# Sampled key-block copies and key high parts: from GpSimd to the activation engine

## The chip, the cores and the metric

The kernel runs on one core of one Trainium2 chip. The metric is the device time of one execution in microseconds, the median of several runs. A profiled execution records every instruction of the engines: TensorE (PE, with its weight loads as PEld), VectorE (DVE), the activation engine (ACT, also ScalarE), GpSimd (POOL) and SyncE (SP, which here issues all DMAs).

## What is computed

A block-sparse attention over 4 batches, 8 heads, 768 positions in 24 blocks of 32, followed by a feed-forward layer with a rational activation. Every query block sees its own block and both neighbours, the first and the last block, and three sampled blocks; query blocks 0 and 23 see all.

```
mask = np.abs(blk_i - blk_j) <= window
mask = mask | (blk_i == 0) | (blk_j == 0) | (blk_i == n_blocks - 1) | (blk_j == n_blocks - 1)
for qb in range(n_blocks):
    for kb in sampled_blocks[qb]:
        mask[qb * block:(qb + 1) * block, kb * block:(kb + 1) * block] = True
scores = np.where(mask, scores, -1000000000.0)
...
h = x @ w_in
P = a[0] + a[1] * h + a[2] * h2 + a[3] * h3
Q = 1.0 + np.abs(b[0]) * np.abs(h) + np.abs(b[1]) * h2
g = P / (Q + 1e-06)
return (g @ w_out).astype(np.float32)
```

## The kernel before

One program interleaves four kinds of work on the engines.

**Keys and queries.** `prep` and `rest` bring the keys of a batch in six pieces of 128x512. ACT takes each piece's largest magnitude (line 384), DVE makes a scale of it (lines 340 to 352), `split16` writes the high part as float16 (`hl`, the operation recorded at line 151 on GpSimd or DVE and at line 147 on ACT), DVE writes the low part (line 378), PE transposes (line 660), and ACT or DVE moves the result to SBUF. For the first batch the result stays in SBUF in `kall`; for the other three it goes to DRAM (`ks`), and each query block's keys are loaded from there by DMA. Queries have a similar chain (`prep_q`, `hlq`).

**Attention.** `attention` handles one query block. In the first batch, the 22 query blocks that are not 0 or 23 need their three sampled key blocks next to each other: `copies` (lines 826 to 829) reads the three block numbers into registers (line 768) and copies three 128x256 float16 slices out of `kall` into one of two buffers `kx`. The two last slots of both buffers hold blocks 0 and 23 and are filled once by `edges` (line 1072). Then come the scores on PE (line 876), the maxima on DVE (886, 915), the exponentials on ACT (904), transposes on PE (945), their evacuation on ACT (147), and the product with the values on PE (1002).

**Weights.** `weights` and `w_scaled` decode the 64-bit weights: a conversion (lines 147 and 151), three DVE steps (434, 437, 440), a maximum on ACT for `w_in`, and a split in high and low parts (498 and 451 on GpSimd). They feed the units.

**Units.** `unit` takes 256 rows of tokens and 256 columns of the hidden layer: PE at lines 1113 to 1115, ACT at 1120, 1124, 1134, 1141 and 1144, DVE at 1127 to 1158, PE again at 1169 to 1171.

All of it is laid out by a planner, `issue`: every step is an `Op` with an engine, an estimated duration in ns, the steps that it follows, a priority, and the buffers that it takes (`Slot`, `Ring`). The planner repeatedly takes the step that can start first by its own estimates and appends its instructions to its engine's queue; engines then run their queues in order. A step made with `among` has a home engine and others; another engine is chosen where it could start earlier than the home engine by more than a fixed amount (243 ns for GpSimd, 534 ns for ACT, 500 ns for DVE).

Of the kernel before, what the change touches and what calls it, by code (L numbers as in the profile page):

```python
# [23 lines left out]
def kernel(  # L24
# [27 lines left out]
    nc = tc.nc  # L52
# [43 lines left out]
    VE, SC, PO, TE, SY = "DVE", "Activation", "Pool", "PE", "SP"  # L96
# [42 lines left out]
    def among(key, home, **prices):  # L139

        d = {{"ve": VE, "sc": SC, "po": PO}[n]: p for n, p in prices.items()}
        return {home: d[home], **(d if key in ALT else {})}
# [181 lines left out]
    o_setup = Op(VE, 5300, setup, [o_small], prio=-70, uses=[s_work])  # L324
# [183 lines left out]
    kall = const.tile([P, NB, H, BLK], F16, name="kall")  # L508
# [27 lines left out]
    s_kall = [Slot(r_kg) for _ in kgs]  # L536
# [78 lines left out]
    def rest(b, w, j, d, o_scale, sc, prio, before):  # L615
        first = b == 0
        t, g = units[j]
        if first:
            s_ld = d["slot"]
            s_ld.left -= 2  # L620
            o_ld = None
        else:
            d, s_ld = {}, Slot(r_ld)

            def load():
                d["ld"] = new_ld(s_ld)
                load_unit((k, v)[w], b, t, g, d["ld"])

            o_ld = before[w] = Op(SY, [(475, 262144)], load, (), prio - 1, takes=[s_ld], behind=before[w])
        s_hl = Slot(r_hl)  # L630

        def high(eng):
            d["hl"] = new_hl()
            split16(d["ld"], sc[0], d["hl"], w, eng)

        def low():
            split16(d["ld"], sc[0], d["hl"], w, None)

        o = Op(among("k", PO, po=671, ve=396, sc=613) if w == 0 else among("K", PO, po=914, ve=600), 0, high, [o_scale, o_ld], prio, takes=[s_hl], uses=[s_ld])
        o = Op(VE, 663 if w == 0 else 800, low, [o], prio, uses=[s_ld, s_hl])  # L640
        if w == 1:
            def store():
                if kv[b][1] is None:
                    kv[b][1] = scr.tile([S, H * 2 * D], F16, name="vs")
                n = HU * 2 * D
                nc.sync.dma_start(out=kv[b][1][t * CH:(t + 1) * CH, g * n:(g + 1) * n].rearrange("(p s) c -> p s c", s=2),
                                  in_=d["hl"].rearrange("p (s j) a d -> p s (j a d)", s=2))
            v_done[b].append(Op(SY, [(650, 262144)], store, [o], prio, uses=[s_hl, s_scr[b]]))
            return
        on_dve = [first and (j, e) in ((0,1),(1,1),(2,1),(3,1),(4,1),(5,1)) for e in range(2)]  # L650
        ring = r_ph if first else r_sp
        s_ps = Slot(ring)
        if g == 0 and not first:
            s_kt[b] = Slot(r_kt)

        def transposes():
            d["pt"] = (ps_h.tile([P, 512], F32, name="ph") if first else ps_s.tile([P, 512], F32, name="sp")).bitcast(F16).rearrange("p (s h n) -> p s h n", s=2, h=HU)
            for e in range(2):
                for h in range(HU):
                    nc.tensor.transpose(d["pt"][:, e, h], d["hl"][:, 2 * h + e].rearrange("p a d -> p (a d)"), ident16)  # L660

        def evac(e):
            def run(eng):
                if g == 0 and e == 0:
                    kts[b, t] = kgs[t] if first else p1.tile([P, KB, H, BLK], F16, name="kt")
                dst = kts[b, t][:, :, g * HU:(g + 1) * HU].rearrange("p b h (r s) -> p s h b r", s=2)[:, e]
                src = d["pt"][:, e].rearrange("p h (b r) -> p h b r", b=KB)
                times(eng, dst, src, 1.0)
            return run

        def store():
            if kv[b][0] is None:
                kv[b][0] = scr.tile([NB, P, H * BLK], F16, name="ks")
            nc.sync.dma_start(out=kv[b][0][t * KB:(t + 1) * KB].rearrange("b p c -> p b c"), in_=kts[b, t].rearrange("p b h r -> p b (h r)"))

        o = Op(TE, 445, transposes, [o], prio, takes=[s_ps], uses=[s_hl])
        sk = s_kall[t] if first else s_kt[b]
        a = Op(among("e", VE if on_dve[0] else SC, sc=478, ve=598), 0, evac(0), [o], prio, takes=[sk] if g == 0 else [], uses=[s_ps] + ([] if g == 0 else [sk]))
        a.behind = k_evac[b, t][0] if g else None
        c = Op(among("e", VE if on_dve[1] else SC, sc=478, ve=598), 0, evac(1), [o, a], prio, uses=[s_ps, sk])  # L680
        k_evac.setdefault((b, t), []).extend([a, c])
        if g == 1 and not first:
            k_done[b].append(Op(SY, [(475, 524288)], store, k_evac[b, t], prio, uses=[sk, s_scr[b]]))
# [81 lines left out]
    def sampled_rows(x, eng=mybir.EngineType.SP):  # L765

        if (x, eng) not in rows_of:
            rows_of[x, eng] = nc.values_load_multi_w_load_instructions(
                ix[0:1, block(parts[x][1]), 0:NR], engines=[eng], min_val=0, max_val=NB - 1,
                skip_runtime_bounds_check_because="clamped when ix was written")[1]  # L770
        return rows_of[x, eng]
# [12 lines left out]
    kxs = early.tile([P, 2, NR + 2, H, BLK], F16, name="kx", bufs=1)  # L784
# [9 lines left out]
    chain = {}  # L794

    def attention(b, j, prio):
# [7 lines left out]
        w, e4 = (c, e2 // XB), e2 % XB  # L804
# [4 lines left out]
        prio = [prio + 0.05 * m for m in range(n)]  # L809
        omax, oexp, onrm = [], [], []  # L810
        prs = {}
        for m, x in enumerate(xs):
            def one(m, x):
                p = prio[m]
# [4 lines left out]
                h = {}  # L819
                if near and n > 1:  # L820
                    deps += [o for t in range(NCH) for o in k_evac[b, t]]
                    kslots = s_kall
                elif near:
                    s_kx = Slot(r_kx)

                    def copies():
                        rows = sampled_rows(x, mybir.EngineType.Pool)
                        for r in range(NR):
                            nc.gpsimd.tensor_copy(out=kxs[:, s_kx.buf, r].rearrange("p h r -> p (h r)"), in_=kall[:, bass.ds(rows[r], 1)].rearrange("p o h r -> p (o h r)"))

                    a = Op(PO, 1500, copies, [o_setup, chain["edges"]], p - 1, takes=[s_kx], uses=s_kall)
                    deps.append(a)
                    kslots = [s_kx] + s_kall
                else:
                    s_kg = Slot(r_kg)

                    def load():
                        kg, ks, = kgs[s_kg.buf], kv[b][0]
                        flat = kg.rearrange("p s h r -> p s (h r)")
                        if n > 1:  # L840
                            nc.sync.dma_start(out=flat, in_=ks[m * NS:(m + 1) * NS].rearrange("b p c -> p b c"))
                            return
                        nc.sync.dma_start(out=flat[:, 0:3], in_=ks[i - 1:i + 2].rearrange("b p c -> p b c"))
                        if h["new"]:
                            nc.sync.dma_start(out=flat[:, 3 + NR:], in_=ks[0:NB:NB - 1].rearrange("b p c -> p b c"))
                        rows = sampled_rows(x)
                        for r in range(NR):
                            nc.sync.dma_start(out=flat[:, 3 + r], in_=ks[bass.ds(rows[r], 1)].rearrange("o p c -> p (o c)"))

                    def price():  # L850
                        h["new"] = fresh("k", x, s_kg)
                        if n > 1:
                            return [(475, 524288)]
                        l = [(475, 196608)] + ([(475, 131072)] if h["new"] else [])
                        return l + [(860, 65536), (560, 65536), (560, 65536)]

                    a = Op(SY, price, load, [o_setup] + k_done[b], p - 1.95, takes=[s_kg], uses=[s_scr[b]], behind=chain.get("kg"))
                    chain["kg"] = a
                    deps.append(a)
                    kslots = [s_kg]  # L860
# [21 lines left out]
                def maxima():  # L882
                    st = d["st"]
                    add = bias[:, i] if n == 1 else bias[:, 0, 0:1].broadcast_to([P, NS])
                    for g in range(2):
# [5 lines left out]
                o = chain["sc"] = Op(TE, 800 if near else 668, scores, deps, p, behind=chain.get("sc"), takes=[s_sp, s_pr] + ([s_st] if m == 0 else []),  # L891
                                     uses=kslots + [Q["slot"]] + ([] if m == 0 else [s_st]))
# [25 lines left out]
        for m, x in enumerate(xs):  # L918
            s_pr, exps = d[m]
            oexp.append(Op(SC, 1172, exps, [omax], prio[m] + 0.1, takes=[G["s_sm"]] if e4 == 0 and m == 0 else [],  # L920
                           uses=[s_pr, s_st, Q["cslot"]] + ([] if e4 == 0 and m == 0 else [G["s_sm"]])))
# [95 lines left out]
        p = prio[-1] + 3 * 0.1  # L1017
# [301 lines left out]
```

## Time and profile before

| | us |
|---|---|
| median of 3 runs | 892.88 (891.15 to 894.04) |
| profiled execution, its own time | 894.15 |
| span of its instructions | 892.0 |
| PE / DVE / ACT / POOL busy | 828.4 / 743.9 / 653.1 / 157.0 |

The span runs from the first to the last recorded instruction. Busy time is the sum of an engine's instructions; a share taken over the whole span mixes stages with different limits, so the tables by stretch are read first. A "releaser" is what ended the idle time before an instruction.

### The profile page before, as it was taken

To read this page: it belongs to the slowest core of one execution; us is meant where nothing else is said; L and a number is where in the kernel's file an instruction comes from. 1 tells how busy PE (TensorE), PEld (TensorE's weight loads), DVE (VectorE), ACT (ScalarE), POOL (GpSimd) and SP (SyncE) were. 2 spreads that over 40 slices of the span, in tenths; PEclk is the share of its full clock that TensorE was granted. 3 is DMA by queue.
4 is the path that set the end of the run, shared out by engine and by line. 5 is a ranking of instruction groups with operands and counts; after the bars stand their busy time and mean duration, and the time that the engine had idled before them with its cause. 6 is when DMAs were issued, how large, how long until landed. Compare 5 with 4: busy or idle time off the path is not lost.

```text
span 892.0 us, 27246 instructions
## 1 busy us (share of the span) xinstructions
PE 828.4 (93%) x10328; PEld 644.8 (72%) x10328; DVE 743.9 (83%) x1824; ACT 653.1 (73%) x1379; POOL 157.0 (18%) x188
## 2 busy tenths in 40 slices
PE   8988586776999999989999999999999999999997
PEld 3555365565778888777887788878888787788885
DVE  5668999979999888869877788988888887788885
ACT  6668666794788787778876887798758587767563
POOL 2434755736420000100000000200000000000000
PEclk9999798688899999999999999999999999999999
DMA  7799788875776976589655975699557556740000
GB/s 204 188 180 219 175 185 172 183 203 161 188 175 160 250 211 155 149 201 240 176 144 149 264 203 161 156 236 240 152 151 183 145 158 161 174 113 25 1 25 24
DMA packets 238482, 148.02 MB, mean 166 GB/s; under 512 B 16016, under 2 KB 222736, under 8 KB 238352
## 3 DMA queue, kind: packets, MB, share of 16 engines
q1 hardware_dynamic: 238352, 146.29, 65.8%
q8 instruction: 82, 1.34, 0.7%
q14 instruction: 48, 0.39, 0.2%
HBM read 128.92 MB, written 11.01 MB: 157 GB/s over the span
## 4 chain that ended last, share of the span: by engine, by line
PE 61%; DVE 8%; ACT 3%; DMA 3%; SPq 2%; issue 1%; ACTq 0%; DVEq 0%
PE ph L1113 8%; PE acc L1169 8%; PE acc L1171 8%; PE acc L1170 8%; PE ph L1114 7%; PE ph L1115 7%; PE av L1002 5%; PE pt L945 4%; PE sp L876 4%; DMA ld<-in_k_dram 1%; DVE gh L1148 1%; DVE ab L1137 1%; PE sp L733 1%; DVE tt L1154 1%; PE sp L1048 1%
## 5 line engine op out<-in xcount | busy, mean ns | idle before, releaser
L1113 PE MATMUL ph<-xh,wi 128*128 128x256 f16 x768 | 213.2, 278 | 3.8 <-DVE tt L1130 2.6
L1115 PE MATMUL ph<-xh,wi 128*128 128x256 f16 x768 | 212.0, 276 | 2.4 <-POOL wi L498 2.4
L1114 PE MATMUL ph<-xl,wi 128*128 128x256 f16 x768 | 212.0, 276 | 1.0 <-DVE xl L1060 1.0
L904 ACT ACTIVATE pr<-pr,st,cq 128x256 f32<-128x256 f32 x224 | 132.2, 593 | 61.0 <-DVE st L915 54.2
L1169 PE MATMUL acc<-wo_h,gh 128*128 128x512 f32 x384 | 164.9, 429 | 0.0
L1171 PE MATMUL acc<-wo_h,gl 128*128 128x512 f32 x384 | 154.7, 403 | 7.3 <-DVE gl L1158 6.6
L1170 PE MATMUL acc<-wo_l,gh 128*128 128x512 f32 x384 | 154.1, 401 | 1.2 <-POOL wo_l L451 1.2
L1120 ACT ACTIVATE sq<-ph,fc 128x512 f32<-128x512 f32 x96 | 65.3, 680 | 60.2 <-PE ph L1115 59.7
L1137 DVE SCALAR_TENSOR_TENSOR ab<-sq,absb,ab 128x512 f32<-128x512 f32 x96 | 74.1, 772 | 34.3 <-ACT ab L1134 34.0
L151 POOL TENSOR_SCALAR hlq<-ldq,scq 128x512 f16<-128x512 f32 x24 | 23.2, 968 | 445.2 <-DVE scq L352 239.5
L1113 PEld LDWEIGHTS <-wi 128*128 128x128 f16 x768 | 76.2, 99 | 32.2 <-issue 16.5
L886 DVE CUSTOM_DVE_ANT_1 pr<-sp,bias 128x256 f32<-128x256 f32 x224 | 84.6, 418 | 13.8 <-PE sp L876 13.4
L1171 PEld LDWEIGHTS acc<-wo_h,gl 128*128 128x128 f32 x384 | 73.6, 192 | 26.6 <-DVE gl L1158 9.3
L1148 DVE SCALAR_TENSOR_TENSOR gh<-tt,par,rr 128x512 fp32r<-128x512 f32 x96 | 74.9, 780 | 17.1 <-PE acc L1170 13.1
L945 PE MATMUL pt<-ident,pr 128*128 128x128 f32 x448 | 77.1, 294 | 11.8 <-ACT pr L904 7.7
L1115 PEld LDWEIGHTS <-wi 128*128 128x128 f16 x768 | 76.1, 99 | 13.8 <-POOL wi L498 2.9
L1169 PEld LDWEIGHTS acc<-wo_h,gh 128*128 128x128 f32 x384 | 73.9, 192 | 15.7 <-issue 1.2
L945 PEld LDWEIGHTS pt<-ident,pr 128*128 128x128 f32 x448 | 67.4, 206 | 24.7 <-ACT pr L904 10.1
L1170 PEld LDWEIGHTS acc<-wo_l,gh 128*128 128x128 f32 x384 | 73.9, 192 | 14.0 <-POOL wo_l L451 1.8
L1114 PEld LDWEIGHTS <-wi 128*128 128x128 f16 x768 | 76.1, 99 | 9.1 <-issue 1.1
L1002 PE MATMUL av<-vg,pT 128*32 128x64 f32 x3584 | 75.1, 226 | 4.7 <-ACT pT L147 2.5
L1002 PEld LDWEIGHTS av<-vg,pT 128*32 128x32 f32 x3584 | 57.1, 112 | 29.5 <-issue 8.9
(140 smaller groups left out, 1669.3 us busy)
## 6 DMA issues: line engine op xcount, KB each, us to landing
vg<-in_v_dram SPq DMA_DIRECT2D x312, 64.0 KB, 3.3
vg<-in_v_dram SPq DMA_DIRECT2D x88, 192.0 KB, 4.1
vg<-in_v_dram SPq DMA_DIRECT2D x24, 512.0 KB, 5.2
kall<-ks SPq DMA_DIRECT2D x52, 192.0 KB, 2.9
kall<-ks SPq DMA_DIRECT2D x156, 64.0 KB, 2.0
ld<-in_k_dram SPq DMA_DIRECT2D x36, 256.0 KB, 5.5
wl<-in_moe_w_in_dram SPq DMA_DIRECT2D x32, 256.0 KB, 4.8
wl<-in_moe_w_out_dram SPq DMA_DIRECT2D x16, 512.0 KB, 4.1
```

The costliest lines, as they stand in the source:

```text
L886: nc.vector.tensor_tensor_reduce(out=prs[x][:, g].rearrange("p (s r) -> p s r", r=BLK), in0=h["sp"][:, g].rearrange("p (s r) -> p s r", r= ...
L904: nc.scalar.activation(out=prs[x][:, g], in_=prs[x][:, g], func=AF.Exp, scale=Q["c"], bias=st[:, 6 + g:7 + g], accum_out=total if n == 1 e ...
L945: nc.tensor.transpose(pp[:, jj * P:(jj + 1) * P], cols, ident)
L1002: nc.tensor.matmul(av[rows, g], pT[:, 2 * g + kt, rows] if plain else pT[:, 2 * g + kt, pa_, rows], vf[:, g * HG + h4, kt * D:(kt + 1) * D ...
L1113: nc.tensor.matmul(o, wh, xh[:, :, cc], start=(cc == 0), stop=False)
L1114: nc.tensor.matmul(o, wh, xl[:, :, cc], start=False, stop=False)
L1115: nc.tensor.matmul(o, wl, xh[:, :, cc], start=False, stop=(cc == NCC - 1))
L1137: nc.vector.scalar_tensor_tensor(out=d["ab"], in0=d["sq"], scalar=absb[:, 1:2], in1=d["ab"], op0=ALU.mult, op1=ALU.add)
L1148: nc.vector.scalar_tensor_tensor(out=d["gh"], in0=d["tt"], scalar=par[:, 0:1], in1=d["rr"], op0=ALU.add, op1=ALU.mult)
L1169: nc.tensor.matmul(acc[:, t], ghs, wo_h[:, f], start=(new and e == 0), stop=False)
L1170: nc.tensor.matmul(acc[:, t], ghs, wo_l[:, f], start=False, stop=False)
L1171: nc.tensor.matmul(acc[:, t], gls, wo_h[:, f], start=False, stop=(last and e == 1))
```

## The change

The copies of the sampled key blocks are made by the activation engine, which also reads the block numbers into its own registers, and the planner's estimate for the three copies goes from 1500 to 1100 ns. The home engine of the keys' high parts becomes the activation engine; GpSimd and DVE stay allowed for them. `edges` stays on GpSimd.

```diff
-        o = Op(among("k", PO, po=671, ve=396, sc=613) if w == 0 else among("K", PO, po=914, ve=600), 0, high, [o_scale, o_ld], prio, takes=[s_hl], uses=[s_ld])
+        o = Op(among("k", SC, po=671, ve=396, sc=613) if w == 0 else among("K", PO, po=914, ve=600), 0, high, [o_scale, o_ld], prio, takes=[s_hl], uses=[s_ld])
...
-                        rows = sampled_rows(x, mybir.EngineType.Pool)
+                        rows = sampled_rows(x, mybir.EngineType.Activation)
                         for r in range(NR):
-                            nc.gpsimd.tensor_copy(out=kxs[:, s_kx.buf, r].rearrange("p h r -> p (h r)"), in_=kall[:, bass.ds(rows[r], 1)].rearrange("p o h r -> p (o h r)"))
-
-                    a = Op(PO, 1500, copies, [o_setup, chain["edges"]], p - 1, takes=[s_kx], uses=s_kall)
+                            nc.scalar.copy(out=kxs[:, s_kx.buf, r].rearrange("p h r -> p (h r)"), in_=kall[:, bass.ds(rows[r], 1)].rearrange("p o h r -> p (o h r)"))
+
+                    a = Op(SC, 1100, copies, [o_setup, chain["edges"]], p - 1, takes=[s_kx], uses=s_kall)
```

## Rows read from the trace of the kernel before

**Rows 1.** Busy us (count) by stretch: PE, PEld, DVE, ACT, POOL; PEclk, DMA, GB/s.

```profile
100.00:120.00 20.00, 13.21 (x225) 10.39 (x225) 19.90 (x46) 13.67 (x30) 12.49 (x17) 0.74 0.52 127
120.00:140.00 20.00, 17.95 (x216) 13.61 (x218) 19.27 (x37) 10.90 (x24) 10.00 (x11) 1.00 0.90 183
140.00:160.00 20.00, 11.47 (x203) 8.27 (x192) 18.85 (x49) 14.76 (x34) 10.57 (x14) 0.74 0.86 194
160.00:180.00 20.00, 15.34 (x172) 11.81 (x170) 19.37 (x43) 14.48 (x30) 17.01 (x15) 0.67 0.78 173
180.00:200.00 20.00, 15.27 (x189) 12.00 (x187) 14.10 (x30) 18.51 (x41) 5.51 (x6) 0.90 0.77 204
240.00:260.00 20.00, 19.31 (x220) 15.06 (x218) 20.00 (x43) 14.46 (x29) 6.44 (x5) 1.00 0.80 164
500.00:600.00 100.00, 99.55 (x1271) 80.35 (x1273) 85.49 (x211) 83.52 (x180) 8.76 (x9) 1.00 0.76 198
```

**Rows 2.** The chain that ended last, us 190 to 200 and 200 to 260: shares by line.

```profile
by line: ACT pr L904 11.7%; ACT scrap L384 9.8%; issue 9.5%; DVE wi L437 6.9%; ACT wi L147 6.7%; DVE pr L886 6.7%; DVE wi L440 6.2%; ACT dw L147 5.7%; DVE wi L434 4.4%; ACT ld L147 0.4%; DVE st L886 0.2%
...
by line: DVE gl L1158 8.7%; DVE tt L1154 7.7%; DVE dw L437 7.2%; DVE gh L1148 7.1%; DVE dw L440 6.7%; DVE ab L1137 6.5%; DMA kall<-ks 5.8%; issue 5.7%; DVE tt L1127 5.5%; DVE ab L1151 5.0%; DVE fc L1087 5.0%; DVE pr L886 4.0%; DVE dw L434 3
```

**Rows 3.** Instructions of the copies, their block numbers' loads, the high parts: ns min/median/max.

```profile
L829 POOL COPY kx<-kall x66: 392/400/952, 27.3 to 182.3; 128x256 f16 x66
L768 POOLq TENSOR_LOAD <-ix x22: 725/730/946, 26.2 to 175.3; - x22
L151 POOL TENSOR_SCALAR hl<-ld,sc x17: 684/1114/1401, 152.1 to 588.9; 128x512 f16<-128x512 f32 x17
L147 ACT ACTIVATE hl<-ld,sc x1: 722/722/722, 372.6 to 372.6; 128x512 f16<-128x512 f32 x1
```

**Rows 4.** The copies alone (line 829) by stretch: us, POOL busy and count.

```profile
20.00:100.00 80.00, 16.26 (x39) 0.98 0.91 201
100.00:180.00 80.00, 14.55 (x24) 0.79 0.76 169
180.00:200.00 20.00, 2.45 (x3) 0.90 0.77 204
```

**Rows 5.** DVE in order of time, us 148 to 157: start us, us, instruction.

```profile
148.70 0.90 DVE L437 SCALAR_TENSOR_TENSOR wi<-wl,wi 128x512 int32<-128x512 int32 x1
149.65 0.76 DVE L440 SCALAR_TENSOR_TENSOR wi<-wl,wi 128x512 int32<-128x512 int32 x1
150.32 0.88 DVE L1154 SCALAR_TENSOR_TENSOR tt<-tt,par,ab 128x512 f32<-128x512 f32 x1
151.81 0.88 DVE L1158 TENSOR_TENSOR gl<-tt,rr 128x512 fp32r<-128x512 f32 x1
153.28 1.17 DVE L378 SCALAR_TENSOR_TENSOR hl<-ld,sc,hl 128x512 f16<-128x512 f32 x1 [0.59 <-POOL hl L151]
154.72 0.74 DVE L378 SCALAR_TENSOR_TENSOR hl<-ld,sc,hl 128x512 f16<-128x512 f32 x1
155.38 0.68 DVE L437 SCALAR_TENSOR_TENSOR wi<-wl,wi 128x512 int32<-128x512 int32 x1
```

**Rows 6.** GpSimd in order of time: beside Rows 5, and at the first weights.

```profile
148.66 3.49 POOL L829 COPY kx<-kall 128x256 f16 x6 [0.99 <-PE sp L876]
152.13 1.79 POOL L151 TENSOR_SCALAR hl<-ld,sc 128x512 f16<-128x512 f32 x2
...
68.62 1.09 POOL L829 COPY kx<-kall 128x256 f16 x3 [3.64 <-PE sp L876]
69.68 2.04 POOL L151 TENSOR_SCALAR dw<-wi,scw 128x512 f32<-128x512 f32 x3
```

**Rows 7.** ACT groups of the whole span by shape: busy us, mean ns.

```profile
L904 ACT ACTIVATE pr<-pr,st,cq 128x256 f32<-128x256 f32 x224 | 132.2, 593 | 61.0 <-DVE st L915 54.2 <-DVE cq L724 6.6
L147 ACT ACTIVATE wi<-dw 128x512 f16<-128x512 f32 x16 | 9.4, 625 | 0.0
```

**Rows 8.** Waits, us 0 to 100: total us, times, longest.

```profile
POOL kx L829 <- PE sp L876: 10.1, 7, 3.9
```

## What the change should do to the time

> **What bounds the kernel now.** I read the busy time by stretch first, because the share over the whole span (PE 93%) mixes two kernels [rows 1]. From about us 260 on PE is never free: 99.55 of 100 us between 500 and 600. What is left to do there is fixed, so the end moves with the moment at which that state is reached. Between 100 and 260 PE is not the limit. DVE is: it is busy 77.39 of the 80 us from 100 to 180 and all 20 of 240 to 260. Between 180 and 200 the picture turns: DVE falls to 14.10 while ACT is busy 18.51 of 20. Second, the chain of waits: from 200 to 260 its named lines are nearly all DVE, from 190 to 200 ACT holds a third of it (exponentials, weight conversion, maxima) [rows 2]. So before us 260 a microsecond taken from DVE is worth up to a microsecond, one added to ACT costs nothing between 100 and 180, where ACT is idle 26.19 us (80 less 53.81), and costs all of itself between 180 and 200. GpSimd is at 5.5 to 17 of 20 us and bounds nothing by its own time.
>
> The third view is the instructions of the copies: 66, of 392 to 952 ns, median 400 [rows 3]. The spread is the interesting part. In order of time, beside the six copies at us 148.66, DVE instructions with two SBUF inputs are longer than the same ones without GpSimd beside them [rows 5, 6]. GpSimd's work thus costs DVE time, though nobody waits for it by name.
>
> **What is removed.** *The copies.* Between 148.7 and 152.7 DVE's line 437 takes 0.90 us against 0.68 at 155.38, line 440 takes 0.76 against that same 0.68, line 1154 takes 0.88 against the 0.74 of the undisturbed three-operand step at 154.72, and line 1158 takes 0.88, which I set against the 0.68 too [rows 5]. The excess is 0.22 + 0.08 + 0.14 + 0.20 = 0.64 us beside six copies, 0.107 us for each. In the DVE-bound stretch and the one after it lie 24 + 3 = 27 copies [rows 4]; 27 x 0.107 = 2.9 us of DVE. The other 39 come before us 100, where DVE has room; nothing is counted for them. Bounds: 0, if DVE merely waits elsewhere, and 27 x 0.40 = 10.8, if every copy held DVE for its undisturbed length. I stay at 2.9, the row that stands beside copies.
>
> The trace shows DVE and GpSimd lengthening each other, and only in some pairs. The Trainium skill (GPSIMD Engine Reference, 8. Key points) says that the two share SBUF interfaces and contend when the DVE instruction has two SBUF inputs or runs in a two-port mode; taken as full exclusion that would give an estimate of 10.8 in place of 2.9 us, and the rows with 0.76 and 0.88 speak for the smaller number.
>
> *The high parts.* Six of the 18 later ones lie between 152 and 180. At 153.28 a DVE low part takes 1.17 us against 0.74 beside two high parts on GpSimd [rows 5, 6]: 0.43 for two, 1.3 us for six. Bounds 0 and 6 x 0.69 = 4.1. The twelve of the batches after that fall in the PE-bound part, where only 0.45 of 100 us are to be had [rows 1]; I take 0.5 us for both, 0 to 0.9. The six of the first batch (before us 24) change engine at about equal price, and are counted at nothing: ACT's evacuations of the transposed keys cover or collide with them, by at most one instruction, 0.72 us either way.
>
> *GpSimd's queue.* The copies at 68.62 had waited 3.64 us for PE's scores, and the scaling of the first weights stands behind them until 69.68 [rows 6]. Over the first 100 us such waits sum to 10.1 us [rows 8]. Freed, those weights start up to 1.1 us sooner. I take nothing, since ACT's own copies then stand in front of ACT's part of the same weights.
>
> **What is added.** *Copies on ACT.* No row shows one. Nearest below: half of a 128x512 conversion of 625 ns, 0.31 us; above: the 128x256 exponential of 593 ns [rows 7]. I take 0.40, the undisturbed length on GpSimd and between the ends; three are 1.2 us. Each group of three needs a load of its block numbers, 730 ns of the queue [rows 3]; on GpSimd it ran while earlier copies did. Bounds 0 and 0.73 for each group; I take 0.2. So 1.4 us for a group (0.93 to 2.5), 22 groups, 31 us on ACT. Eight groups, 11.2 us, fall between 100 and 180 into 26.19 us of idle ACT: cost nothing, as long as they find the gaps. One, at 180, falls where ACT is the limit: 1.4 us on the path. In front of us 100 are 13 groups, 18 us; the ends of that stretch are DMA arrivals, and I count nothing.
>
> For the copy itself the Trainium skill (VectorE: DVE Perf Modes, The TRN2 errata) gives ScalarE 224 cycles and one for each element at 1.2 GHz from SBUF to SBUF, an estimate of 0.40 us; no run shows it yet, and the sum would be the same by it.
>
> *High parts on ACT.* 722 ns for the one that ACT already does, against 684 to 1401 on GpSimd [rows 3]. The six take 4.3 us of the same idle 26.19: 15.5 with the copies. GpSimd is chosen whenever it can start 243 ns sooner, so some will stay there; the gain of 1.3 shrinks with them.
>
> *The new wait.* A copy waits until PE has done with its buffer. On GpSimd those 10.1 us [rows 8] held up GpSimd alone. On ACT, whatever is queued behind waits too: exponentials and evacuations, for which PE waits, and conversions and maxima of the weights, for which DVE waits.
>
> **The sum.** Gains 2.9 + 1.3 + 0.5 = 4.7, cost 1.4, net 3.3 us. The profiled time of 894.15 becomes 890.85 (span 888.7). That execution lies 1.27 above the median of 892.88, so the median becomes 889.6, 0.37% faster. About 0.3%, 2.7 us, is what a measurement of this kernel can tell from no change.
>
> **The rivals.** *ACT becomes the bound: slower.* Place: us 100 to 200. ACT's idle time there is broken into pieces that come before results of DVE; a group of 1.4 us, put ahead of something that DVE needs, delays DVE, which has only 2.61 idle us in 80 to catch up. At stake are 11.2 + 4.3 + 1.4 = 16.9 us. Where half of it is exposed, 8.45 less the gain of 4.7 is 3.75 us: 896.6. Where all of the copies are and no high part, 12.6 - 4.7 = 7.9: 900.8. It decides from 4.7 / 16.9 = 28% exposure on. For it: ACT at 67% goes to 87% of 100 to 180 (15.5 more in 80), and queues run in order. Against it: ACT stays below DVE's 97%, and the planner knows the 1100 ns.
>
> *The gain is given back: no difference.* The planner finds ACT fuller and hands weight conversions to GpSimd, which lengthens DVE again. At 0.215 us each (0.43 for two) ten conversions return 2.2 of the 3.3 us: 891.8. For it: GpSimd has just been freed.
>
> *The high parts don't move.* ACT is rarely free within 243 ns, and nearly all 18 stay on GpSimd. The gain is 1.8 smaller: 891.4, no measurable difference. It is possible because the edit changes a preference alone.
>
> *DVE is freed by more.* If copies held DVE at twice the row's rate, 2.9 more: 886.7. It counts with the forecast, as faster.
>
> **How the numbers follow.** Forecast 0.40, of which 0.10 with the larger relief; ACT as the bound 0.30; given back 0.18; high parts unmoved 0.12. Hence faster 0.40, within 0.3% 0.30, slower 0.30: two mechanisms of nearly equal size stand against each other, and which one wins is not much better than open. The range for the measured time is 884 to 901: the low end takes 2.9 more for the copies and some of the weights and the high parts' upper bound; the high end is that of all copies exposed. The likeliest case's own range is 886 to 891.5.
>
> **What would show it.** The profile after should have 66 ACT copies of about 0.40 us, GpSimd busy some 35 to 55 us less than 157, and DVE's lines 437, 440, 1154 and 1158 with fewer long instances between 100 and 180. The forecast is right if DVE stays above 95% there and PE reaches its full state about 3 us sooner. It is wrong if DVE's idle time between 100 and 200 grows beyond the 8.5 us of now, with ACT's exponentials, conversions or evacuations as the releasers, or if copies on ACT wait for PE's scores with those behind them. If GpSimd's busy time falls by less than the copies' 33 us, work has come back to it.

## The result, and the profile after

The changed kernel takes 888.87 us (median; 885.71 to 893.16) against 894.05 of the kernel before: ratio 0.9935, 95% interval 0.9911 to 0.9959. A second measurement, among the experiments, gave 0.9906 (0.9875 to 0.9937). Both intervals lie below 1: it is faster, by 0.65% and 0.94%; 0.37% was forecast.

The first profile is of the longest of the nine executions (893.16 us), so the readings below are from the second, of 887.19 us. The page first: the span, and each engine's busy us and instructions.

```profile
span 885.4 us, 27256 instructions
...
PE 825.7 (93%) x10349; PEld 645.1 (73%) x10349; DVE 738.2 (83%) x1825; ACT 672.5 (76%) x1444; POOL 118.9 (13%) x122
```

GpSimd has 38 us less than 157.0, ACT 19 us more than 653.1, DVE 5.7 us less than 743.9. The first profile has a span of 891.4 us and the same busy time of DVE, 738.2: the two profiles of this one kernel end 6.0 us apart. Next the copies, the loads of their block numbers and the high parts of the later batches, which answer to [rows 3] (ns min/median/max, first and last start).

```profile
L829 ACT COPY kx<-kall x66: 388/402/419, 26.7 to 195.2; 128x256 f16 x66
...
L768 ACTq TENSOR_LOAD <-ix x22: 696/702/2027, 25.1 to 192.4; - x22
...
L147 ACT ACTIVATE hl<-ld,sc x5: 698/706/724, 157.3 to 563.0; 128x512 f16<-128x512 f32 x5
...
L151 POOL TENSOR_SCALAR hl<-ld,sc x13: 692/857/1964, 168.3 to 582.1; 128x512 f16<-128x512 f32 x13
```

On ACT all copies are alike, 388 to 419 ns, where they ranged from 392 to 952 on GpSimd. Of the 18 later high parts five are now on ACT, where one was before, and of the first batch's six two: GpSimd has lost six high parts in all. In turn the weights' conversions went the other way: in the groups of line 151 GpSimd now makes 25 of them (wo_h 9, wi 8, dw 8), seven more than before.

Last the busy time by stretch, for [rows 1] (PE, PEld, DVE, ACT, POOL, then PEclk, DMA, GB/s); the last line is of the kernel before.

```profile
100.00:180.00 80.00, 54.03 (x874) 43.97 (x873) 73.50 (x167) 66.56 (x155) 34.94 (x30) 0.92 0.89 192
180.00:200.00 20.00, 20.00 (x206) 15.83 (x204) 17.48 (x44) 15.95 (x37) 3.42 (x5) 0.88 0.59 164
200.00:260.00 60.00, 50.08 (x660) 38.45 (x657) 60.00 (x136) 44.78 (x95) 25.39 (x21) 0.94 0.67 183
...
200.00:260.00 60.00, 51.01 (x578) 39.04 (x577) 59.77 (x129) 38.32 (x79) 29.24 (x23) 0.89 0.69 176
```

Between 100 and 260 DVE is idle for 6.5 + 2.52 + 0 = 9.0 us, against 2.61 + 5.90 + 0.23 = 8.7 before: not less. ACT rose from 53.81 to 66.56 in the first 80 us and fell from 18.51 to 15.95 in the 20 after them.

### The profile page after: what moved, and what is told of

The parts are those of the page before. It is cut to its first block, busy times and chain, and to the rows that moved or that the text cites. A ratio compares the mean times of both kernels' runs of the same rounds, so it can differ in the third digit from the quotient of the medians.

```text
span 891.4 us, 27256 instructions
## 1 busy us (share of the span) xinstructions
PE 826.2 (93%) x10349; PEld 645.1 (72%) x10349; DVE 738.2 (83%) x1825; ACT 672.4 (75%) x1444; POOL 119.8 (13%) x122
## 4 chain that ended last, share of the span: by engine, by line
PE 60%; DVE 13%; DMA 11%; SPq 6%; ACT 5%; issue 3%; POOL 1%; ACTq 0%; POOLq 0%; DVEq 0%
PE acc L1169 8%; PE ph L1113 8%; PE acc L1171 7%; PE acc L1170 7%; PE ph L1115 7%; PE ph L1114 7%; PE av L1002 5%; PE pt L945 4%; PE sp L876 4%; DMA ldq<-in_q_dram 4%; DMA vg<-in_v_dram 3%; DVE tt L1127 1%; DMA ld<-in_k_dram 1%; ACT scrap L384 1%; SPq L972 1%
## 5 line engine op out<-in xcount | busy, mean ns | idle before, releaser
L1115 PEld LDWEIGHTS <-wi 128*128 128x128 f16 x768 | 75.6, 98 | 9.7 <-POOL wi L498 0.4
```

The source lines that it names most:

```text
L1115: nc.tensor.matmul(o, wl, xh[:, :, cc], start=False, stop=(cc == NCC - 1))
```

## The experiments

**What was asked.** The prediction takes the gain from work that changes engines, which relieves DVE (theory 1 in the expectations). A rival to that arose with the result: the planner lays out everything anew for any change of its inputs, and of two programs with the same work one may simply have the better plan (theory 2). Theory 3 says that GpSimd's queue, freed of the copies, has the weights ready sooner. An engine can be exchanged without touching the plan: the step is planned as before and only its instructions go into another queue. That separates the two.

**The two halves of the change.** The copies alone:

```diff
 among("k", PO, po=671, ve=396, sc=613)
-nc.gpsimd.tensor_copy(...)
+nc.scalar.copy(...)
-Op(PO, 1500, copies, ...)
+Op(SC, 1100, copies, ...)
```

> The copies go to the activation engine, the key high parts keep GpSimd as home; the planner lays the program out anew. Theory 1 (DVE is relieved of GpSimd's copies): most of the gain is here, 2.9 of 4.7 us by the prediction, so 0.994 to 0.998 of the kernel before. Theory 2 (the gain comes from the order that the planner happened to make): any value between 0.99 and 1.01, unrelated to the share of GpSimd work removed. Theory 3 (GpSimd's queue is freed, weights are ready sooner): like theory 1, with the first unit's matmuls at least 1 us sooner than 81.5 us.

Measured 1.0057 (1.0035 to 1.0079). The half that should have held most of the gain makes the kernel slower.

The high parts alone:

```diff
-among("k", PO, po=671, ve=396, sc=613)
+among("k", SC, po=671, ve=396, sc=613)
```

> Only the home engine of the key high parts changes; the copies stay on GpSimd. Theory 1 (relief of DVE): small, at most 1.8 us of gain, and less as only a few high parts move: 0.998 to 1.000. Theory 2 (order): any value between 0.99 and 1.01, as the planner's order changes throughout for an edit that moves a handful of instructions.

Measured 0.9890 (0.9858 to 0.9922): a gain as large as the whole change's within the intervals, from the half that takes six instructions of 0.7 us off GpSimd. Neither result fits the sum. Theory 2 had set 0.99 to 1.01 for both: the first lies in it, the second just below it by its median. So wide a range is weak support; the exchanges that follow decide more.

**The engine exchanged, the plan kept.** First, copies on ACT in the plan of the kernel before:

```diff
-nc.gpsimd.tensor_copy(...)
+nc.scalar.copy(...)
 Op(PO, 1500, copies, ...)
```

> The copies are issued on the activation engine, but the planner still plans them as GpSimd steps of 1500 ns with GpSimd as home of the high parts: the queues of PE, DVE and SyncE keep exactly the order of the kernel before, only the copies and their register loads sit in ACT's queue at the place where they were planned for GpSimd. Theory 1 (relief of DVE by fewer GpSimd instructions): 1 to 4 us faster than before, 0.9955 to 0.999, DVE busy time down by 3 to 4 us. Theory 2 (the order of the changed kernel is what is faster): no gain, 1.000 to 1.008, as the order is the old one and ACT has 27 us more to do. Rival of the prediction (copies block ACT): slower by over 0.3%, with ACT idle before the copies until PE's scores.

Measured 1.0011 (0.9985 to 1.0037): no gain that can be told. Then copies on GpSimd in the plan of the changed kernel:

```diff
-nc.scalar.copy(...)
+nc.gpsimd.tensor_copy(...)
 Op(SC, 1100, copies, ...)
```

> The reverse: the order of the changed kernel on PE, DVE and SyncE to the instruction, high parts placed as in the changed kernel, but the copies are issued on GpSimd. Theory 1 (relief): the gain of the copies is gone, the time lies 2 to 4 us above the changed kernel, 0.996 to 1.000 of the kernel before. Theory 2 (order): the gain stays or grows, since ACT is also spared 27 us: 0.985 to 0.994 of the kernel before. Theory 3 (GpSimd's queue): above the changed kernel by 2 us or more, with scaling of weights on GpSimd late behind the copies.

Measured 0.9939 (0.9915 to 0.9964). The plan of the changed kernel, with its moved high parts, brings a gain with the copies where they were before; against 0.9935 and 0.9906 of the changed kernel itself, the engine of the copies makes no difference that these intervals can tell. They don't exclude one of up to about 3 us (0.9939 less 0.9906). Theory 3 falls as well: in this run the first unit's matmuls start at 72.0 us, as in the changed kernel (72.1) and not as in the kernel before (81.5), though the copies stand in GpSimd's queue.

```profile
L1113 PE MATMUL ph<-xh,wi x768: 269/273/421, 72.0 to 877.1; 128*128 128x256 f16 x192
...
L1113 PE MATMUL ph<-xh,wi x768: 269/273/422, 72.1 to 868.1; 128*128 128x256 f16 x192
...
L1113 PE MATMUL ph<-xh,wi x768: 269/273/421, 81.5 to 874.7; 128*128 128x256 f16 x192
```

The lines are this run's, the changed kernel's and that of the kernel before. The earlier first weights are the plan's doing, not the freed queue's.

**The changed kernel again,** without an edit, beside the next three:

> The changed kernel once more, on the same chip and against the same runs of the kernel before as the three next to it, with a new profile. If the gain is a property of the program: 0.991 to 0.996 again. The new profile should show in which stretch of the span the gain lies; the first profile, at 893.16 us, was the longest of nine executions.

Measured 0.9906 (0.9875 to 0.9937), a little more than was expected. The gain is a property of the program.

**Another plan, no engine changed by the edit.** One estimate of the planner in the kernel before:

```diff
-a = Op(PO, 1500, copies, ...)
+a = Op(PO, 1400, copies, ...)
```

> Kernel before with one number changed: the planner's estimate for the three copies on GpSimd is 1400 instead of 1500 ns. No work changes its engine, no instruction is added or removed but PE's filling matmuls; only the order of the queues comes out otherwise. Theory 2 (the order decides, as a lottery): the time moves by more than 0.3% either way, within 0.985 to 1.01. Theory 1 (engines' work decides): 0.998 to 1.002.

Measured 1.0102 (1.0071 to 1.0134). And one constant of the planner's choice:

```diff
-slack, fend, f00, fgap = 21.0, 80000, 3000, 0
+slack, fend, f00, fgap = 25.0, 80000, 3000, 0
```

> Kernel before with one constant of the planner changed: of two steps the one of smaller priority is preferred if it starts at most 25 ns (21 before) later. No work changes engine by edit; a second sample of what another order alone does. Theory 2 (order as a lottery): off by more than 0.3% in either direction, within 0.985 to 1.015. Theory 1 (engines' work alone decides): 0.998 to 1.002.

Measured 1.0080 (1.0047 to 1.0113). Neither edit says that any work changes its engine; only the planner's free choices (order, and the engine of the steps that may go to several) come out otherwise (GpSimd has 182 and 187 instructions in these runs, 188 before). They cost 1.0% and 0.8%, and in both cases the change is far larger than the 0.2% that theory 1 allowed. What a plan costs shows in the stretches of the first one's profile:

```profile
100.00:180.00 80.00, 56.20 (x840) 43.94 (x843) 74.97 (x164) 53.49 (x117) 46.82 (x52) 0.81 0.83 165
180.00:200.00 20.00, 12.05 (x136) 9.47 (x126) 16.60 (x24) 15.03 (x30) 6.67 (x5) 0.74 0.78 219
200.00:260.00 60.00, 49.90 (x561) 38.04 (x562) 54.68 (x132) 40.87 (x86) 26.28 (x23) 0.89 0.63 173
```

DVE's idle time from 100 to 260 is 5.03 + 3.40 + 5.32 = 13.75 us, against 8.7 before and 9.0 after, so this plan loses 5 us in the stretch that DVE bounds. Its longest waits from 180 to 262 have no common cause; below the three dots stand two of the kernel before:

```profile
DVE wi L434 <- ACT wi L147: 2.1, 1, 2.1
DVE gh L1148 <- PE acc L1170: 1.8, 1, 1.8
DVE dw L434 <- ACT dw L147: 1.8, 1, 1.8
...
DVE dw L434 <- ACT dw L147: 2.2, 1, 2.2
DVE wi L434 <- ACT wi L147: 1.6, 1, 1.6
```

Each comes once. The waits for conversions on ACT stand in the kernel before too, in sum as long (3.8 and 3.9 us), so the 5 us aren't theirs; the wait at line 1148 is new, and some below 1 us. The last unit's matmul shows where it ends up, at 884.7 us here, 868.1 in the changed kernel and 874.7 in the kernel before.

The gains don't follow TensorE's granted clock either. Its mean (1 is full speed) over the executions is 0.968 in the kernel before beside the first four experiments, 0.971 in the slower run of the copies alone, and 0.970 in the faster one of the high parts alone.

**The copies left out.** In the kernel before and in the changed one, each in its own plan, 60 of the 66 copies and 20 of the 22 loads of their block numbers are omitted, so the later query blocks use wrong sampled keys:

```diff
-rows = sampled_rows(x, ...)
-for r in range(NR):
+rows = sampled_rows(x, ...) if s_kx.buf not in filled else ()
+for r in range(NR if s_kx.buf not in filled and not filled.add(s_kx.buf) else 0):
```

> Kernel before in its own order, with 60 of the 66 copies and 20 of the 22 register loads on GpSimd left out: each of the two buffers is filled once and then stands, so later query blocks see wrong sampled keys. It prices the copies on GpSimd. Theory 1 (relief of DVE): 3 to 5 us faster, 0.994 to 0.997, with DVE's busy time down by about 4 us. If the copies on GpSimd cost the end nothing: 0.999 to 1.001, though DVE's busy time is down by the same.

Measured 0.9966 (0.9944 to 0.9987): in the kernel before, the copies with their loads cost 3.0 us (0.34% of 893; 1.2 to 5.0 by the interval). Page of this run:

```profile
PE 826.9 (93%) x10328; PEld 643.0 (72%) x10328; DVE 740.1 (83%) x1824; ACT 654.6 (74%) x1379; POOL 124.9 (14%) x128
```

DVE is busy for 3.8 us less, without having one instruction less. The two exchanges of the engine say the same of DVE, each within one plan: 741.4 us with the copies on ACT against 743.9 in the old plan, 738.2 against 740.8 in the new one. The relief of DVE is real, and has the size of the prediction's term (2.9). Its place is the forecast one too: DVE's queue has the same order with and without the copies, and set against each other one by one, the instructions that start between 100 and 200 are 2.4 us shorter in sum without them, those before 100 0.8 us, all of them 2.9.

> Changed kernel in its own order, with 60 of the 66 copies and 20 of the 22 register loads on ACT left out in the same way. It prices the copies on ACT: by the prediction 1.4 us below the changed kernel, so 0.990 to 0.995 of the kernel before; if ACT's extra work is exposed (the rival), 4 to 8 us below the changed kernel, 0.984 to 0.990.

Measured 0.9908 (0.9877 to 0.9940), beside 0.9906 with the copies. On ACT, in the changed kernel's plan, they cost nothing that these intervals can tell (0.3% each way). In the plan of before they seem to: there the copies on ACT came to 1.0011, on GpSimd to 1, and without them to 0.9966. So unplanned on ACT they cost about as much as on GpSimd, 0.45% against 0.34%, a difference that is within the intervals.

**The high parts' engine,** with the plan of the run that changed their home alone:

```diff
-split16(d["ld"], sc[0], d["hl"], w, eng)
+split16(d["ld"], sc[0], d["hl"], w, nc.gpsimd)
```

> The program of the run with the high parts alone changed, its order of PE and SyncE to the instruction, but the seven high parts that the planner gave to ACT or DVE are issued on GpSimd, which then makes all 24 as in the kernel before. If the engine of the high parts matters: 1 to 2 us above that run, 0.990 to 0.994 of the kernel before. If that run's gain is its order: the same as it within its interval, 0.986 to 0.992.

Measured 0.9942 (0.9916 to 0.9968). Half of that run's gain stays with all high parts on GpSimd, so that half is its plan. (The kernel before had one of the 24 on ACT.) The median lies just above the range set for either case, and nearer to the one in which their engine matters. The other half, 0.5%, may belong to their engine; the intervals touch, and DVE's busy time is 744.5 us in both profiles, so no relief of DVE shows. It stays open, and no run puts the high parts back in the changed kernel's plan: how its 0.6% with the copies on GpSimd is shared between plan and high parts is not shown.

**GpSimd's two-input steps.** If a step on GpSimd costs DVE time, the costliest should be the 32 subtractions that make the weights' low parts. In the changed kernel's plan they are issued on DVE:

```diff
-eng.tensor_tensor(out=wo_l[:, x], ...)
+nc.vector.tensor_tensor(out=wo_l[:, x], ...)
...
-eng.tensor_tensor(out=wi[:, x, u, 1], ...)
+nc.vector.tensor_tensor(out=wi[:, x, u, 1], ...)
```

> Changed kernel in its own order of PE, ACT and SyncE, with the 32 two-input subtractions of the weights' low parts issued on DVE instead of GpSimd (16 of line 451, 16 of line 498). If GpSimd's two-input steps cost DVE about what the overlap count says (22 us of lengthening for 46 us of GpSimd), DVE's own 32 x 0.69 = 22 us replaces that, and the time stays within 3 us of the changed kernel: 0.990 to 0.997 of the kernel before. If the lengthening is not a loss for DVE (it would be idle anyway), the 22 us come on top in the DVE-bound stretch: 1.005 to 1.02.

Measured 0.9879 (0.9845 to 0.9913), 885.07 us: faster than either case had it, though the interval overlaps with that of the changed kernel. The groups, and the page's line of engines:

```profile
L451 DVE TENSOR_TENSOR wo_l<-dw,wo_h 128x512 fp32r<-128x512 f32 x16 | 11.2, 701 | 0.6 <-POOL wo_h L151 0.6
L498 DVE TENSOR_TENSOR wi<-dw,wi 128x512 f16<-128x512 f32 x16 | 11.1, 697 | 0.9 <-ACT wi L147 0.9
...
PE 826.7 (94%) x10349; PEld 645.1 (73%) x10349; DVE 734.3 (83%) x1857; ACT 672.0 (76%) x1444; POOL 75.8 (9%) x90
```

DVE has 11.2 + 11.1 = 22.3 us of new work and is busy for 3.9 us less than in the changed kernel (738.2). As busy time the rest has thus shrunk by 26 us; recorded instructions overlap a little at their ends, and added up one by one the other 1825 are shorter by 22 us. On GpSimd the same steps took 1493 and 1403 ns each:

```profile
L451 POOL TENSOR_TENSOR wo_l<-dw,wo_h 128x512 fp32r<-128x512 f32 x16 | 23.9, 1493 | 17.9 <-ACT wo_h L147 17.2
L498 POOL TENSOR_TENSOR wi<-dw,wi 128x512 f16<-128x512 f32 x16 | 22.3, 1403 | 3.9 <-ACT wi L147 3.9
```

46.2 us of GpSimd were paid for by DVE with 22 to 26 us, about as much as DVE needs to do the work itself, or more.

**Both together:** the plan with the high parts' home changed, copies on GpSimd, the subtractions on DVE.

> The order of the run with the high parts alone changed, copies on GpSimd, and the 32 subtractions of the weights' low parts on DVE as in the last run. If the two gains add: 0.983 to 0.987 of the kernel before, below both kernels and about equal to the last run. If the copies on GpSimd cost DVE 3 us here as in the kernel before, it stays 2 to 3 us above the sum: 0.986 to 0.990. If the subtractions only fit the other order: 0.990 or more.

Measured 0.9848 (0.9817 to 0.9879), 882.97 us: the lowest median of all and below both kernels, though its interval overlaps with that of the run before it. It lies in the range set for gains that add, and it does not need the half of the change that moves the copies.

## Why the prediction was right, and where it was not

The direction was right, and both measurements lie in the range (884 to 901) and below the forecast's 889.6 by less than a us. That closeness is luck: the forecast went down by 3.3 us from 892.88, the median of three executions, while the kernel before took 894.05 and 897.59 beside the two measurements, which lie 5.2 and 8.6 us below it. The sum that led there, though, is not the account of the gain.

**The step that failed is the sum's silent assumption** that everything outside the diff stays where it was. The prediction priced each moved instruction, and its rivals too were made of moved instructions; the planner appears only as knowing an estimate, or as handing conversions back. The runs show what a new plan is worth by itself: minus 0.6% (the changed kernel's plan with the copies still on GpSimd, though with its six moved high parts), minus 0.6% (the high parts' plan with all of them still on GpSimd), plus 0.8% and plus 1.0% (edits of the planner's numbers). That is a term of 5 us down to 9 us up, against a priced net of 3.3 us. It would also account for the copies' half alone being slower; that plan was not run with its copies on GpSimd, so this is not shown. The term belonged in the range as a cost that no row shows, and in the chances as a rival for both signs; instead the chance of slower went to ACT as the bound.

**Copies on GpSimd, 2.9 us of DVE:** right in size and place: 3.8 us of DVE's busy time (added up by instruction 2.9, of which 2.4 between 100 and 200, where 2.9 were forecast), and 3.0 us of the end. The lengthening read off four instructions beside six copies gave the size for all, with some luck in the parts: of the lines read, 437 and 1158 lose their instances of over 0.85 us between 100 and 180 (three and two) when the copies are left out, 440 and 1154 keep two each. The rival that doubled the term is not borne out.

**Copies on ACT, 1.4 us on the path and 0.40 us each:** 0.402 each, as taken. The estimate of 0.40 us from the Trainium skill (VectorE: DVE Perf Modes, The TRN2 errata) agrees with it. The term of 1.4 us was too high: leaving the copies out changed nothing that can be told. The last group still stands between 180 and 200, at 194.6, but ACT is busy for 15.95 of 20 us there now and is not the limit. The loads of the block numbers, 702 ns, ran for 16.1 of their 17.1 us while ACT worked.

**High parts, 1.3 and 0.5 us:** mis-sized. All 18 were counted, and GpSimd lost four of them. The rival that foresaw this (chance 0.12) was right that most would stay; that the 243 ns decided it is not shown. What the moved ones are worth stays open: 0.5% by the medians in the other plan, with no relief of DVE to be seen.

**Conversions handed back to GpSimd:** happened, seven of the ten supposed; what they cost was not measured by itself.

**ACT as the bound:** it does not show in the changed kernel, where ACT is busy 66.56 of 80 us. It may show where the copies are put on ACT without being planned there: DVE is relieved (741.4 us against 743.9), and yet no gain can be told.

**What should have shown it:** that DVE stays above 95% from 100 to 180 was wrong (73.50 of 80, 92%), and its idle time up to 260 didn't fall. From 100 to 200 it even grew from 8.5 to 9.0 us, the first half of the prediction's own sign of being wrong; the second isn't there, as the longest wait is for PE (2.4 us at line 1148), not for ACT. Where the gain lies isn't settled. PE is busy for 196.05 of the 200 us from 400 to 600 in the profiled execution of the kernel before and for 198.34 in the changed kernel, but for 198.40 in that of the slower plan with the other constant, the fastest of its seven executions. One sign is common to the plans that gain: in all eight profiles of the changed kernel's plan and of the high parts' plan the first unit's matmuls start between 71.3 and 75.6 us, in the six of the other plans between 77.9 and 85.1. It is a sign and no shown cause; the two profiles of the changed kernel start at 71.3 and 72.1 and end 6.0 us apart.

## What to carry to other kernels

Where a planner lays out the program, split every change into the new plan and the new work: issue the old work in the new plan and the new work in the old one, and shift one harmless estimate to see how far a plan alone moves the time. Without these controls a gain below about 1% here can't be put down to the edit that came with it. Price a GpSimd step by what it does to DVE, not by its own idle time: read the lengthening off the instructions beside it.

## What the runs showed of the hardware

The subtractions on GpSimd cost DVE about as much as doing them itself, or more: 32 of 128x512 with two inputs, 46.2 us on GpSimd, lengthened DVE by 22 to 26 us, while DVE does them in 22.3. The one-input 128x256 copies cost far less, 3.8 us of DVE for 60 of them, 0.06 us each. The two kinds differ in inputs, size and type, and no run tells which of these makes the difference.

GpSimd pays as well: its 66 copies took 33.3 us in the kernel before, against 26.4 at their undisturbed 0.40 each. The prediction cited the Trainium skill (GPSIMD Engine Reference, 8. Key points) for the contention of the two. If DVE stood still for the undisturbed length of every copy, that would be 60 x 0.40 = 24 us; the measured 3.8 us decides against it. For the subtractions it is 22 to 26 of 46.2 us.
